# Batch 0 cut into query parts of 256 and 320 rows in place of 384 and 192, and its feed-forward rows divided at 255 in place of 256

## The chip, the cores and the metric

The kernel runs on 1 core of one Trainium2 chip. The metric is the device time of one execution in microseconds (us), lower is better. Engines are named as in the profile: PE is TensorE (PEld its weight loads), DVE is VectorE, ACT is ScalarE, POOL is GpSimd, SP is SyncE, which issues the DMAs.

## The reference, cut to what matters

Top-k attention, then a gated feed-forward block with a convolution of three taps along the sequence. There are 8 batches, 8 heads, 576 rows, 64 columns per head, 32 kept scores; the feed-forward block has 512 model columns and 1024 inner ones.

```python
scores = scale * np.matmul(q, k.transpose(0, 1, 3, 2))
kth = np.partition(scores, -top_k, axis=-1)[..., -top_k:-top_k + 1]
scores = np.where(scores >= kth, scores, -1000000000.0)
attn = np.exp(scores - np.max(scores, axis=-1, keepdims=True))
x = np.matmul(attn / (np.sum(attn, axis=-1, keepdims=True) + 1e-09), v)   # heads side by side: (B, S, 512)
h = np.maximum(x @ w_in, 0.0)
conv_out = sum(conv_w[k] * hp[:, k:k + S, :] for k in range(3))            # hp: h with a zero row at both ends
out = (h * (1.0 / (1.0 + np.exp(-conv_out)))) @ w_out
```

## The kernel before, in words

**Tiles.** Heads go in pairs. The 576 queries of a batch are four blocks of 128 and one of 64. A tile is 128 query rows against all 576 keys for one head (the 64-row blocks of two pairs share tiles), so a batch has 36 tiles and the program 288. `PARTS` (line 65) gives the order inside a batch: blocks 0, 1, 2 for all four pairs (24 tiles), then block 3 and the 64 for all four pairs (12 tiles).

**The order of the work.** A Python loop, `iteration(it)`, writes the instructions of PE, ACT, DVE and POOL in their final order; each call is one tile step, with many tiles in flight. A tile n passes: scores on PE, then `evacuate` (ACT, L252) two steps before `chunk_ops` reads it; `chunk_ops` and `cand_ops` (DVE, L268 to L290: the largest values of seven pieces of the row); `sides` (ACT, L302); `flip` (POOL, L307, writes the tile's z); one step later `expo` (ACT, L314, which takes its shift from z); and one more step later `below` (DVE, L317, which reads z), `select` (DVE, L321) and `weigh` (DVE, L335); then transposes and products with v on PE. SP's DMAs are ordered by the framework's own scheduler.

**Weights.** In the first 33 steps the 64-bit weights are fetched in 33 blocks (block 0 the taps, 1 to 16 of w_in, 17 to 32 of w_out) and converted, one block a step: DVE cuts them (L162, then one step later L171), ACT works on them between (L165, L167), POOL ends the conversion (L176, L178, L179).

**Shared buffers.** Two rings of six buffers each, tags `x_hi` and `x_lo` of the pool `xp`, hold both the raw weight blocks of `load` (line 143, ten blocks ahead of use) and later the attention outputs of `normalise` (line 420: L424, L425 `x_hi`, L426 `x_lo` on POOL). Whoever takes a buffer waits until its last reader is done.

**Feed-forward.** `ROWS` (line 89) divides a batch's 576 rows into a group of 256 and one of 320. When all four pairs of a part are normalised, `ffn` queues 8 expansions (`Expand`: 12 matmuls, L456; the convolution on POOL, L489 to L503; tanh on ACT, L517; the gate on DVE, L525) and the contractions (`Contract`: a split of 128 rows on POOL, L588 and L592; matmuls L613). The first group needs one row more than it holds, since the convolution reaches a row further: 257 rows (258 columns are computed), for which two blocks don't do. Credits (`FEED`, `LEAN`, `PACE`, `FIRST`) set how many of these units a step takes. The last units run after the last tile.

```python
PARTS = ((0, 1, 2), (3, None))
ROWS = [(0, NI * TAIL), (NI * TAIL, S)]
feed = EARLY if state.blocks < BLOCKS else FEED if work[min(max(it, 0), NT - 1)].pc.part == 0 else LEAN
```

## Time and profile before

| What | Value |
|---|---|
| median of 3 runs | 1099.97 us (1098.80 to 1101.86) |
| the profiled execution | 1099.58 us, of which the span of the program is 1097.8 us |
| busy: DVE, PE | 1031.1 us (94%), 1022.0 us (93%) |
| busy: ACT, POOL | 956.1 us (87%), 934.0 us (85%) |
| DVE busy from 50 to 200 us | 149.65 of 150 us |
| mean granted TensorE clock of the span | 0.983 of full speed |

The profiled execution's own time is 1.8 us over its span, which leaves out what lies around the program. Sums further down are made against 1099.58 us. Shares of busy time are means over stages with different limits: a part with weight conversion, a long even part, and a tail without tiles, so a stretch is to be read by itself.

### The profile page before, as it was taken

To read this page: it belongs to the slowest core of one execution; us is meant where nothing else is said; L and a number is where in the kernel's file an instruction comes from. 1 tells how busy PE (TensorE), PEld (TensorE's weight loads), DVE (VectorE), ACT (ScalarE), POOL (GpSimd) and SP (SyncE) were. 2 spreads that over 40 slices of the span, in tenths; PEclk is the share of its full clock that TensorE was granted. 3 is DMA by queue.
4 is the path that set the end of the run, shared out by engine and by line. 5 is a ranking of instruction groups with operands and counts; after the bars stand their busy time and mean duration, and the time that the engine had idled before them with its cause. 6 is when DMAs were issued, how large, how long until landed. Compare 5 with 4: busy or idle time off the path is not lost.

```text
span 1097.8 us, 27626 instructions
## 1 busy us (share of the span) xinstructions
PE 1022.0 (93%) x7890; PEld 761.9 (69%) x7890; DVE 1031.1 (94%) x5792; ACT 956.1 (87%) x2417; POOL 934.0 (85%) x1224
## 2 busy tenths in 40 slices
PE   6777798999989999999999999999999999999997
PEld 3444476766767777776777777776777767776895
DVE  7999999999999999999999999999999999999670
ACT  6888899989999998989999998989999999899551
POOL 6879779988889989899989989899988989899610
PEclk9988899999999999999999999999999999999999
DMA  9241222123212222222311322312311332221101
GB/s 298 90 127 65 69 60 79 48 78 116 72 48 79 85 70 79 77 74 86 96 44 60 119 64 65 94 57 93 93 59 49 98 95 63 65 69 45 40 19 43
DMA packets 71154, 85.96 MB, mean 78 GB/s; under 512 B 12848, under 2 KB 45904, under 8 KB 70992
## 3 DMA queue, kind: packets, MB, share of 16 engines
q1 hardware_dynamic: 70992, 84.10, 24.4%
q8 instruction: 65, 1.06, 0.4%
q14 instruction: 97, 0.79, 0.2%
HBM read 74.48 MB, written 9.58 MB: 77 GB/s over the span
## 4 chain that ended last, share of the span: by engine, by line
PE 57%; DVE 29%; ACT 10%; issue 1%; POOL 1%; DMA 0%; SPq 0%; ACTq 0%; POOLq 0%; DVEq 0%
PE mc L613 13%; PE me L456 12%; PE pt L347 9%; PE mixed L379 8%; DVE cand L268 8%; PE s L246 7%; DVE e L335 7%; DVE z L317 5%; DVE cand L290 2%; ACT weights_ps L314 2%; ACT side L302 2%; PE mixed L382 2%; DVE g L525 2%; PE mixed L230 2%; DVE rows L288 2%; PE weights_ps L613 2%
## 5 line engine op out<-in xcount | busy, mean ns | idle before, releaser
L268 DVE MAX8 cand<-rows 128x8 f32<-128x82 f32 (+1 forms) x2016 | 481.7, 241 | 0.0
L307 POOL TENSOR_TENSOR z<-rows,side 128x579 f32<-128x579 f32 x288 | 347.5, 1207 | 63.2 <-ACT side L302 55.6
L314 ACT ACTIVATE weights_ps<-rows,z 128x576 f32<-128x576 f32 x288 | 220.1, 764 | 22.2 <-DVE e L335 11.8
L335 DVE SCALAR_TENSOR_TENSOR e<-rows,kth,weights_ps 128x576 f32<-128x576 f32 x288 | 231.6, 804 | 0.3
L456 PE MATMUL me<-x_hi,wi 128*128 128x258 f32 (+1 forms) x952 | 227.4, 310 | 2.9 <-ACT g L470 2.8
L302 ACT ACTIVATE side<-rows 128x576 bf16<-128x576 f32 x288 | 223.5, 776 | 0.0
L347 PEld LDWEIGHTS pt<-ident,e 128*128 128x128 f32 x1152 | 123.7, 143 | 139.8 <-issue 21.1
L317 DVE MAX8 z<-z 128x8 f32<-128x576 f32 x288 | 213.9, 743 | 0.0
L613 PE MATMUL mc<-wo,split 128*128 128x512 f32 x732 | 199.2, 404 | 0.5 <-ACT o L629 0.5
L347 PE MATMUL pt<-ident,e 128*128 128x128 f32 x1152 | 193.0, 291 | 5.4 <-DVE e L335 5.0
L355 ACT COPY pT<-pt 128x512 f32<-128x512 f32 x256 | 153.1, 598 | 45.4 <-PE pt L347 44.9
L246 PE MATMUL s<-k,q 64*128 64x512 f32 x512 | 169.9, 671 | 3.1 <-ACT rows L252 3.0
L252 ACT COPY rows<-s 128x512 f32<-128x512 f32 x288 | 166.7, 579 | 5.7 <-PE s L246 4.2
L379 PE MATMUL mixed<-pT,vn 128*64 128x128 f32 (+1 forms) x2560 | 167.1, 275 | 0.0
L456 PEld LDWEIGHTS me<-x_hi,wi 128*128 128x128 f32 x952 | 161.8, 189 | 4.3 <-ACT g L470 4.3
L379 PEld LDWEIGHTS mixed<-pT,vn 128*64 128x64 f32 x2560 | 132.3, 141 | 17.4 <-issue 1.4
L613 PEld LDWEIGHTS mc<-wo,split 128*128 128x128 f32 x732 | 128.6, 189 | 21.6 <-POOL t L503 0.7
L456 PE MATMUL me<-x_lo,wi 128*128 128x258 f32 (+1 forms) x476 | 142.0, 298 | 0.0
L489 POOL TENSOR_SCALAR t<-g,cr 128x256 f32<-128x256 f32 (+1 forms) x228 | 116.5, 511 | 0.0
L288 DVE MAX8 rows<-cand 128x8 f32<-128x21 f32 x576 | 106.3, 185 | 0.0
L503 POOL TENSOR_TENSOR t<-t,t 128x256 f32<-128x256 f32 (+1 forms) x114 | 91.4, 802 | 9.5
L456 PEld LDWEIGHTS me<-x_lo,wi 128*128 128x128 f32 x476 | 90.9, 191 | 0.0
(126 smaller groups left out, 1695.7 us busy)
## 6 DMA issues: line engine op xcount, KB each, us to landing
vn<-in_v_main_dram SPq DMA_DIRECT2D x64, 256.0 KB
k<-in_k_dram SPq DMA_DIRECT2D x32, 384.0 KB
k<-in_k_dram SPq DMA_DIRECT2D x32, 352.0 KB
out_dram<-o SPq DMA_DIRECT2D x26, 256.0 KB
q<-in_q_dram SPq DMA_DIRECT2D x32, 192.0 KB
rb<-row SPq DMA_DIRECT2D x64, 96.0 KB
q<-in_q_dram SPq DMA_DIRECT2D x32, 160.0 KB
raw<-in_w_in_dram SPq DMA_DIRECT2D x16, 256.2 KB
```

The source lines that it names most:

```text
L246: nc.tensor.matmul(s_ps[h], lhsT=qx[d, at:at + P], rhs=kx[d, keys], start=True, stop=True)
L252: nc.scalar.copy(out=x[:, at:at + MAIN], in_=s_ps[t.h])
L268: yield lambda c=c, at=at, n=n: nc.vector.max(out=t.cand[:, c:8 * CHUNKS:CHUNKS], in_=t.x[:, at:at + n])
L302: nc.scalar.activation(out=t.side[:, 2:S + 2], in_=t.x, func=AF.Sign, scale=-OVER, bias=t.row[:, 7:8], accum_out=t.cnt)
L307: nc.gpsimd.tensor_tensor(t.z[:, 8:S + 11], t.row[:, 6:S + 9], t.side, ALU.mult)
L314: nc.scalar.activation(out=e_ps, in_=t.x, func=AF.Exp, scale=scale, bias=t.shift)
L317: nc.vector.max(out=t.z[:, 0:8], in_=t.z[:, 10:S + 10])
L335: nc.vector.scalar_tensor_tensor(out=t.e, in0=t.x, scalar=kth[:, t.n:t.n + 1], in1=e_ps, op0=ALU.is_ge, op1=ALU.mult, accum_out=t.pc.sums[ ...
L347: nc.tensor.transpose(tp[:, i * P:(i + 1) * P], t.e[:, o + i * P:o + (i + 1) * P], ident)
L379: nc.tensor.matmul(a[r, 0:st.w], lhsT=st.pc.vn[:, h, i], rhs=st.unit.pT[:, st.half[h], i, c], start=(i == 0), stop=False)
L456: nc.tensor.matmul(mm[:, 0:w], lhsT=wt, rhs=xx, start=(n == 0), stop=(n == len(ops) - 1))
L613: nc.tensor.matmul(mm[0:m], lhsT=x[:, i], rhs=wo[:, e, f], start=start, stop=stop)
```

## The change

Batch 0 alone gets another plan, `OPENING`: blocks 0 and 1 for all four pairs first (16 tiles), then blocks 2, 3 and the 64 (20 tiles). Its feed-forward rows are divided at 255: a group of 255 rows, which with one row more needs exactly the 256 of the two blocks, and one of 321. A contraction of 128 rows may now take its rows from two groups (127 of the first and 1 of the second for rows 128 to 255 of batch 0), and the next batch's first group waits for that contraction's split as well. Other batches stay as they were. Lines of the changed kernel are 15 to 20 higher: L186 is the L171 of before, L193 and L194 are L178 and L179, L323 is L307, L333 is L317, L337 is L321, L351 is L335, L440 to L442 are L424 to L426, L472 is L456.

```diff
 PARTS = ((0, 1, 2), (3, None))
+OPENING = ((0, 1), (2, 3, None))
...
-    ROWS = [(0, NI * TAIL), (NI * TAIL, S)]
+    CUT = {PARTS: NI * TAIL, OPENING: 2 * P - 1}
+    def parts_of(b):
+        return OPENING if b == 0 else PARTS
+    def rows_of(b, part):
+        return [(0, CUT[parts_of(b)]), (CUT[parts_of(b)], S)][part]
...
     def fetch(pc):
-        last = None in PARTS[pc.part]
+        last = pc.part == 1
         for nm, src, a, z, w in (("k", k, 0, S + 3 * TAIL if last else S + 2 * TAIL, S + 3 * TAIL),
-                                 ("q", q, pc.c0, S + P if last else pc.c1, WIDE)):
+                                 ("q", q, pc.c0, MAIN + P if last else pc.c1, max(WIDE, QW))):
...
-            s_lo, s_hi = ROWS[part]
+            s_lo, s_hi = rows_of(b, part)
...
-            if self.two:
-                srcs = [(0, TAIL, ends[self.b][:, fs]), (TAIL, P, self.gs["g"][:, fs, c0:c0 + TAIL])]
-            else:
-                srcs = [(0, P, self.gs["g"][:, fs, c0:c0 + P])]
+            srcs = [(0, TAIL, ends[self.b][:, fs])] if self.two else []
+            a, r = TAIL if self.two else 0, self.r
+            for gs, part, n in self.of:
+                c0 = gs["at"] + r - rows_of(self.b, part)[0]
+                srcs.append((a, a + n, gs["g"][:, fs, c0:c0 + n]))
+                a, r = a + n, r + n
...
-        if any(o.part == e.part and o.b < e.b for o in unready) or (state.it < state.due and not tail):
+        if any(e.part in o.parts and o.b < e.b for o in unready) or (state.it < state.due and not tail):
...
-        for part, blocks in enumerate(PARTS):
+        for part, blocks in enumerate(parts_of(b)):
```

**POOL, while weights are converted.** Here z is a tile's flipped row, xt a pair's attention output, x_hi and x_lo its two halves in the shared rings, scratch and wo belong to a weight block, and a name's number is its buffer or tile. Before, from the conversion of block 22 on:

```order
L176 TENSOR_TENSOR scratch_130<-scratch_130 128x256 [waits DVE_49]
L178 TENSOR_SCALAR wo_64<-scratch_130 128x256 [waits Pool_49]
L179 TENSOR_TENSOR wo_64<-scratch_130,wo_64 128x256 [waits Pool_49]
L307 TENSOR_TENSOR z_1202<-rows_108,side1_113 128x579 [waits DVE_49,Activation_49]
L424 TENSOR_TENSOR xt0_542<-xt0_542,rb_929 128x384 [waits DMAHW5_49,DMAHW4_49]
L176 TENSOR_TENSOR scratch_130<-scratch_130 128x256 [waits DVE_49]
L178 TENSOR_SCALAR wo_64<-scratch_130 128x256 [waits Pool_49]
L179 TENSOR_TENSOR wo_64<-scratch_130,wo_64 128x256 [waits Pool_49]
L307 TENSOR_TENSOR z_1253<-rows_108,side0_109 128x579 [waits DVE_49,Activation_49]
L425 TENSOR_SCALAR x_hi_1196<-xt0_542 128x384 [waits DMAHW6_49]
```

And in the changed kernel, where the first batch's second pair is normalised, from the conversion of block 21 on:

```order
L191 TENSOR_TENSOR scratch_130<-scratch_130 128x256
L193 TENSOR_SCALAR wo_64<-scratch_130 128x256 [waits Pool_49]
L194 TENSOR_TENSOR wo_64<-scratch_130,wo_64 128x256 [waits Pool_49]
L323 TENSOR_TENSOR z_1181<-rows_108,side0_109 128x579 [waits DVE_49,Activation_49]
L441 TENSOR_SCALAR x_hi_1005<-xt0_766 128x256 [waits DVE_49,Activation_49]
L442 TENSOR_TENSOR x_lo_1006<-xt0_766,x_hi_1005 128x256 [waits DMAHW7_49,DMAHW1_49,Pool_49]
L191 TENSOR_TENSOR scratch_130<-scratch_130 128x256
L193 TENSOR_SCALAR wo_64<-scratch_130 128x256 [waits Pool_49]
L194 TENSOR_TENSOR wo_64<-scratch_130,wo_64 128x256 [waits Pool_49]
L323 TENSOR_TENSOR z_1234<-rows_108,side1_113 128x579
```

The normalisation of the first pairs moved forward by some six conversions, and its x_hi now waits for DVE and ACT. Which instruction it waits for is told by the count in the built program: x_hi_1003 and x_lo_1004, of the first pair, lie where raw blocks 20 and 21 lay, and x_hi_1005 lies where raw64_682 lay, block 24, three blocks ahead of the block 21 that POOL has just converted; it waits for L186 of block 24 on DVE. Before, x_hi_1196 took the place of block 22, which POOL had converted ahead of it.

**DVE, at that L186.** The rows of the changed kernel from L186 of block 24 (raw64_682) to the reading of z_1234, the z that stands behind the waiting x_hi on POOL; cand, second and hot are a tile's largest values, mc and e2 go with a weight block and a tile's exponentials:

```order
L186 SCALAR_TENSOR_TENSOR scratch_130<-raw64_682,mc_131 128x256 [waits Activation_49]
L304 MAX rows_108<-cand_1199 128x8 [waits DVE_49]
L284 MAX cand_1250<-rows_108 128x8
L177 TENSOR_SCALAR mc_131<-raw64_727 128x256 [waits DMAHW5_49,DVE_49]
L337 SCALAR_TENSOR_TENSOR hot_1269,kth_67<-weights_ps_97,cnt_1126,z_1181 128x10 [waits Activation_49]
L351 SCALAR_TENSOR_TENSOR e2_1224,sums_1153<-rows_108,kth_67,weights_ps_97 128x576 [waits DVE_49,PE_49]
L304 MAX rows_108<-cand_1250 128x8 [waits DVE_49]
L306 MATCH_REPLACE cand_1250<-rows_108,cand_1250 128x21 [waits DVE_49]
L333 MAX z_1234<-z_1234 128x8 [waits Pool_49]
```

(Repeated L284 rows between them are left out.) The order of these rows is that of before; what moved is the POOL row that L333 waits for, which now stands behind a wait for L186.

**What does not move.** On each of the four engines the first pass of the two programs is the same list of instructions from one place on: on DVE from its 1413th row in both, after the same 84 tiles; the rows ahead of that place are the same kinds and counts in both but for widths. On DVE 12 gates of 256 columns and 7 of 320 become 7 of 255, 5 of 256 and 7 of 321, which are 5312 columns in both. POOL has four small operations more (2 casts and 2 differences of 128 by 4). On PE the first expansion stands after 26 groups of tile transposes in place of 32.

## Rows read from the trace of the kernel before

**Rows 1.** The page: the span, and the busy time of the engines.

```profile
span 1097.8 us, 27626 instructions
PE 1022.0 (93%) x7890; PEld 761.9 (69%) x7890; DVE 1031.1 (94%) x5792; ACT 956.1 (87%) x2417; POOL 934.0 (85%) x1224
```

**Rows 2.** Busy time by stretch: the stretch in us, its length, busy us (and instructions) of PE, PEld, DVE, ACT, POOL, the mean granted TensorE clock (1.00 is 2.4 GHz), the DMA engines' busy share and GB/s.

```profile
50.00:100.00 50.00, 36.16 (x224) 22.46 (x224) 49.93 (x271) 44.55 (x115) 41.01 (x54) 0.82 0.27 82
100.00:150.00 50.00, 39.62 (x317) 27.36 (x315) 49.86 (x290) 43.91 (x113) 37.97 (x49) 0.87 0.29 91
150.00:200.00 50.00, 46.45 (x408) 36.16 (x405) 49.86 (x290) 47.83 (x124) 47.71 (x70) 1.00 0.17 52
200.00:250.00 50.00, 47.41 (x352) 33.49 (x352) 49.23 (x284) 45.54 (x112) 45.17 (x53) 1.00 0.25 77
250.00:300.00 50.00, 48.38 (x411) 36.33 (x409) 49.25 (x290) 46.27 (x123) 44.05 (x60) 1.00 0.30 95
1050.00:1100.00 50.00, 40.33 (x197) 33.94 (x195) 16.95 (x35) 15.10 (x32) 0.00 (x0) 0.96 0.10 34
```

**Rows 3.** The waits of DVE (who waited, for whom, us in total, times, the longest): one row from 7.5 to 200 us, then two from 200 to 330 us.

```profile
DVE mc L162 <- DMA raw<-in_w_in_dram: 1.7, 1, 1.7
DVE hot L321 <- ACT weights_ps L314: 0.6, 1, 0.6
DVE hot L321 <- ACT weights_ps L517: 0.5, 1, 0.5
```

**Rows 4.** The timeline at the start (start us, duration us, engine, line, operation, and in brackets the idle time before and what ended it), and the page's slices with what the DMAs moved, 27.4 us each.

```profile
1.19 0.42 SPq L211 DMA_DIRECT2D q<-in_q_dram  x1
7.36 0.43 DVE L162 TENSOR_SCALAR mc<-raw 128x256 uint32<-128x256 uint32 x1 [1.66 <-DMA raw<-in_w_in_dram]
9.47 0.43 DVE L171 SCALAR_TENSOR_TENSOR scratch<-raw,mc 128x256 uint16<-128x256 uint16 x1
10.05 0.73 POOL L176 TENSOR_TENSOR scratch<-scratch 128x256 uint32<-128x256 uint32 x1 [3.95 <-DVE scratch L171]
...
GB/s 298 90 127 65 69 60 79 48 78 116 72 48 79 85 70 79 77 74 86 96 44 60 119 64 65 94 57 93 93 59 49 98 95 63 65 69 45 40 19 43
```

**Rows 5.** The timeline of POOL around a conversion and a normalisation.

```profile
91.77 0.51 POOL L425 TENSOR_SCALAR x_hi<-xt 128x384 fp32r<-128x384 f32 x1
92.24 0.73 POOL L176 TENSOR_TENSOR scratch<-scratch 128x256 uint32<-128x256 uint32 x1
...
94.24 1.20 POOL L307 TENSOR_TENSOR z<-rows,side 128x579 f32<-128x579 f32 x1
95.40 1.00 POOL L426 TENSOR_TENSOR x_lo<-xt,x_hi 128x384 fp32r<-128x384 f32 x1
```

**Rows 6.** The timeline of DVE: L171 of block 24, then a later tile step (that of rows 5) and the next.

```profile
82.63 0.42 DVE L171 SCALAR_TENSOR_TENSOR scratch<-raw,mc 128x256 uint16<-128x256 uint16 x1
...
94.21 0.43 DVE L171 SCALAR_TENSOR_TENSOR scratch<-raw,mc 128x256 uint16<-128x256 uint16 x1
96.83 0.74 DVE L317 MAX8 z<-z 128x8 f32<-128x576 f32 x1
98.04 0.43 DVE L171 SCALAR_TENSOR_TENSOR scratch<-raw,mc 128x256 uint16<-128x256 uint16 x1
98.96 0.22 DVE L321 SCALAR_TENSOR_TENSOR hot<-weights_ps,cnt,z 128x10 f32<-128x10 f32 x1
100.71 0.74 DVE L317 MAX8 z<-z 128x8 f32<-128x576 f32 x1
```

**Rows 7.** The timeline of ACT in that tile step.

```profile
95.59 0.43 ACT L167 ACTIVATE scratch<-raw 128x256 uint32<-128x256 uint32 x1
96.33 0.75 ACT L314 ACTIVATE weights_ps<-rows,z 128x576 f32<-128x576 f32 x1 [0.30 <-DVE e L335]
```

**Rows 8.** Groups of POOL with shapes kept apart (busy us, mean ns of one | idle us before).

```profile
L426 POOL TENSOR_TENSOR x_lo<-xt,x_hi 128x384 fp32r<-128x384 f32 x32 | 32.2, 1005 | 2.5
L426 POOL TENSOR_TENSOR x_lo<-xt,x_hi 128x192 fp32r<-128x192 f32 x32 | 19.5, 610 | 1.8
L425 POOL TENSOR_SCALAR x_hi<-xt 128x384 fp32r<-128x384 f32 x32 | 16.5, 516 | 0.0
L425 POOL TENSOR_SCALAR x_hi<-xt 128x192 fp32r<-128x192 f32 x32 | 11.6, 364 | 2.2
L588 POOL TENSOR_SCALAR split<-ends 128x256 fp32r<-128x256 f32 x6 | 2.4, 404 | 0.0
L465 POOL MEMSET g<- 128x8 f32 x8 | 0.9, 114 | 0.0
```

**Rows 9.** Short stretches with the granted TensorE clock, columns as in rows 2.

```profile
115.00:120.00 5.00, 5.00 (x32) 3.57 (x30) 5.00 (x28) 3.90 (x12) 4.34 (x7) 0.57 0.02 5
120.00:125.00 5.00, 3.10 (x21) 2.53 (x21) 5.00 (x30) 4.82 (x13) 3.57 (x6) 0.78 0.27 77
125.00:130.00 5.00, 3.51 (x30) 1.98 (x26) 5.00 (x31) 3.46 (x11) 2.06 (x3) 0.88 0.46 136
130.00:135.00 5.00, 4.10 (x35) 2.65 (x35) 4.93 (x31) 4.89 (x13) 4.52 (x6) 1.00 0.49 158
```

**Rows 10.** Expansions on PE: the first matmul of the first one in the timeline, and 12 matmuls of one unit in the chain that ended last (start us, us).

```profile
140.32 0.36 PE L456 MATMUL me<-x_hi,wi 128*128 128x258 f32 x1
1036.11 1.44 PE s L456 x12
```

More of the change, by code (lines that the diff above doesn't have):

```diff
@@ L75, in attend_and_feed @@
     exact = finish is None
+    pt_bufs = PTB - 1 if exact else PTB
     v_main, v_tail = v
@@ L88, in attend_and_feed, with width @@
     scale = 1.0 / float(D) ** 0.5
-    ROWS = [(0, NI * TAIL), (NI * TAIL, S)]
-    SMAX = max(e - a for a, e in ROWS)
-    WIDE = max(sum(TAIL if i is None else P for i in blocks) for blocks in PARTS)
-    SUMS = 2 * max(sum(1 if i is None else 2 for i in blocks) for blocks in PARTS)
+    CUT = {PARTS: NI * TAIL, OPENING: 2 * P - 1}
[3 more added lines that the diff above has]
+        return [(0, CUT[parts_of(b)]), (CUT[parts_of(b)], S)][part]
+    def width(blocks):
+        return sum(TAIL if i is None else P for i in blocks)
+    PLANS = (PARTS, OPENING)
+    WIDTHS = [max(width(plan[part]) for plan in PLANS) for part in range(2)]
+    WIDE = max(WIDTHS)
+    QW = max(MAIN + P - width(plan[0]) for plan in PLANS)
+    GROUPS = [max(CUT.values()), S - min(CUT.values())]
+    SMAX = max(GROUPS)
+    SUMS = 2 * max(sum(1 if i is None else 2 for i in blocks) for plan in PLANS for blocks in plan)
     const = ctx.enter_context(tc.tile_pool(name="const", bufs=1))
@@ L243, in scores @@
                     r = slice(half_of(one, h) * D, (half_of(one, h) + 1) * D)
-                    nc.tensor.matmul(s_ps[one.h][r], lhsT=qx[d, at:at + TAIL], rhs=kx[d, keys], start=True, stop=True)
+                    c = at + half_of(one, h) * TAIL
+                    nc.tensor.matmul(s_ps[one.h][r], lhsT=qx[d, c:c + TAIL], rhs=kx[d, keys], start=True, stop=True)
                 else:
@@ L461, in emit @@
             if self.f == 0:
-                g = self.gs["g"] = moe.tile([P, NFT, n + 4], F32, name=f"g{self.part}")
+                g = self.gs["g"] = moe.tile([P, NFT, GROUPS[self.part] + 4], F32, name=f"g{self.part}")
                 self.gs["at"] = at
@@ L549, in attend_and_feed, with __init__ @@
         m = P
-        def __init__(self, b, part, s0, half, gs, box):
-            self.b, self.part, self.s0, self.gs, self.box = b, part, s0, gs, box
-            self.two = ROWS[part][1] - ROWS[part][0] - s0 == TAIL
+        def __init__(self, b, r, half, pieces, box):
+            self.b, self.r, self.of, self.box = b, r, pieces, box
+            self.all = [gs for gs, _, _ in pieces]
+            self.parts = [part for _, part, _ in pieces]
+            self.two = r + TAIL == S
             nf = NFT * TAIL // self.m
@@ L619, in emit @@
             m, mm = self.m, self.box.mm
-            r = ROWS[self.part][0] + self.s0
+            r = self.r
             if state.it > NT + 4:
@@ L641, in split_next @@
         c = next((c for c in unready if not hasattr(c, "hi")), None)
-        if c is None or c.gs.get("done", 0) < NFT or (state.late_splits >= 4 if state.it > NT + 4 else state.splits >= SPB):
+        if c is None or any(gs.get("done", 0) < NFT for gs in c.all) or (state.late_splits >= 4 if state.it > NT + 4 else state.splits >= SPB):
             return False
@@ L645, in split_next @@
         return True
+    groups = {}
     def ffn(b, part):
-        gs = {}
+        gs = groups[b, part] = {}
         expands.extend(Expand(b, part, f, gs) for f in range(NFT))
-        n = ROWS[part][1] - ROWS[part][0]
-        for s0 in range(0, n, P):
+        lo, hi = rows_of(b, part)
+        for r in range(lo // P * P, S if part else hi // P * P, P):
+            if S - r == TAIL and b % 2 == 0:
+                unready.append(Keep(b, r, gs))
+                continue
+            pieces = [(gs, part, min(r + P, S) - max(r, lo))]
+            if r < lo:
+                pieces.insert(0, (groups[b, 0], 0, lo - r))
             box = Box()
-            if n - s0 == TAIL and b % 2 == 0:
-                unready.append(Keep(b, part, s0, gs))
-                continue
-            units = [Contract(b, part, s0, half, gs, box) for half in range(2)]
+            units = [Contract(b, r, half, pieces, box) for half in range(2)]
             contracts.extend(units)
```

18 lines of the change are left out of this document (9 added, 9 removed).

## The prediction

> **What bounds the kernel now.** I read the page's busy times first, then the busy time by stretch, then the waits of DVE, and last the order of the two programs. The page has DVE and PE close together, 94% and 93% of a span of 1097.8 us [rows 1], which names neither. The stretches do: from 50 to 200 us DVE is busy for all but 0.35 of 150 us while PE has 3.5 to 14 us free in each 50, and from 200 to 300 us DVE is still at 49.2 of 50 [rows 2]. The waits say the same: after the first weight block has landed, DVE waits for nothing worth a row until 200 us, and from there to 330 us for ACT alone, 0.6 and 0.5 us [rows 3]. Only in the last 50 us does PE carry the end alone [rows 2]. So ahead of 330 us a change is worth what it does to DVE's list of work and to DVE's waits, and nothing else.
>
> The change touches only that part. From the place after 84 tiles the four engines hold the same instructions in the same order in both programs, and ahead of it DVE has the same kinds and counts, its gates the same 5312 columns. The earlier start of batch 0's feed-forward work is thus given back: the next batch's work must wait for it, and by tile 84 both programs have done the same. The tail at the end is the same list, so an early gain on PE buys nothing there. What is left is one new wait, a smaller first transfer, and the clock of PE.
>
> **The change part by part.**
>
> *DVE's work: 0.* Same columns, same counts. DVE was never idle there, so the work can't be packed tighter either: what it could win back is the 1.1 us that it waits for ACT between 200 and 330 us [rows 3]. I take 0, because those waits follow how ACT's tanh and exponentials fall, which the change shifts without thinning; the bound is a gain of 1.1.
>
> *The moved normalisation: about +2.2 us.* The moved x_hi of the second pair lies where raw weight block 24 lay, and so waits for L186 of that block, three conversions ahead of where POOL is. Behind it on POOL, which works in order, stand x_lo, the conversion of block 22 and the next tile's z. Let time 0 be the end of that L186. I price what POOL then still has to do before that z, from rows of before:
> - waking POOL after DVE's L171: 9.47 + 0.43 = 9.90 to 10.05, 0.15 [rows 4];
> - x_hi and x_lo, 256 wide: between 364 and 516 ns, and between 610 and 1005 ns, for 192 and 384 [rows 8]; a third of the way up is 0.41 and 0.74, less some 0.04 that neighbours overlap (x_hi took 0.51, the next began after 0.47 [rows 5]): 0.37 and 0.70;
> - the conversion: 92.24 to 94.24, 2.00 [rows 5];
> - z: 1.20 [rows 5].
>
> The sum is 4.42. DVE reads a z 2.19 after L171's end (94.64 to 96.83 [rows 6]). So L333 comes 2.2 us late, and since DVE has no idle time to take that out of before 200 us, the end is 2.2 us later.
>
> Does it stop there? The next z is due one tile step on, 3.88 later (96.83 to 100.71 [rows 6]), and POOL needs 2.00 + 1.16 for it, so POOL is 0.7 ahead again. ACT's exponential, which takes its shift from the same z, waits as well: it would start 1.69 after time 0 (96.33 [rows 7]) and starts at 4.4, but its reader, L321, follows L317 by 2.13 [rows 6], thus at 6.5, and the exponential of 0.75 has ended at 5.2. ACT's last conversion operation of a block (L167) needs the scratch buffer that POOL frees at 3.2, ahead of the exponential. So one late z, once. The first pair's x_hi and x_lo wait also (for blocks 20 and 21), but POOL has z's in hand then: z follows at 0.15 + 0.70 + 2.00 + 1.20 = 4.05 after block 21's L186, and DVE wants it one whole step and 2.19 later, at 6.0. Nothing.
>
> The bounds: 0, if the buffer were free when POOL comes (nearest rows: x_hi of before follows its z without idle time [rows 5]); 4.4, if DVE had no step in hand and lost all that POOL does after the wait. I take 2.2, from rows of the very step.
>
> *The first transfer: -0.2.* Queries of the first pair shrink from 384 to 256 columns, 66 KB, and the weight block that ends DVE's last early wait lands behind them [rows 4]. At 298 GB/s of the first slice [rows 4] that is 0.2 us; bounds 0 and 0.35, the wait being partly latency.
>
> *Four small POOL operations: 0.* Each lies between the 114 ns of a small memset and the 404 ns of a cast of 256 [rows 8], 0.5 to 1.6 us in all; they fall past 250 us, where POOL has 5.9 of 50 us free [rows 2], with z's due a step later. With that cover gone they would cost up to 1.6.
>
> *SP: 0.* The DMA of the last weight block now waits for block 22's L186, and behind it on SP stand the second pair group's row sums and the keys of the fourth pair of the second part. Those keys are wanted some five tile steps of 3.83 us later (94.21 to 98.04 [rows 6]), far beyond the one step of waiting. The norms' rows are needed on POOL steps later, too.
>
> *Expansions six tiles earlier: 0 on DVE.* Their first matmul moves from 140.3 us [rows 10] to about 140.3 - 6 x 3.83 = 117 us. PE has room in 100 to 150 us [rows 2]; what is uncertain is its clock, below.
>
> Sum: 1099.58 + 2.2 - 0.2 = **1101.6 us** against the profiled execution, which lies 0.4 under the median of the runs (1099.97). That is 0.2% slower; a measurement of this kernel tells about 0.3%, 3.3 us, from no change, so I forecast no difference that can be told.
>
> **The rivals.**
> 1. *Slower: PE falls behind at 1.2 GHz.* The expansions now begin where the granted clock is 0.57 with PE busy 5.00 of 5.00 us [rows 9]. A unit of 1.44 us at full clock [rows 10] is 2.9 at half. Units come every 1.4 tile steps (`FIRST`), 5.4 us, so three begin before the clock is 1.00 at 130 us [rows 9]: 8.6 us against the two tile steps, 7.7 us, by which scores are evacuated ahead of DVE. It decides from the fourth unit at half clock; with five, 14.4 - 7.7 = 6.7 us are lost and the time is 1108.3. For it: 0.57. Against: the rows behind, 0.78, 0.88, 1.00, with less work than there will be. Chance 0.08.
> 2. *Slower: the late z is not made good.* ACT, held 2.7 us, makes the following tiles' rows late as well, and DVE loses twice: 4.4, 1103.8 and a little over. Against: ACT's 5 to 6 us free in 50 [rows 2]. Chance 0.08.
> 3. *No effect at all:* the wait ends in time, or what it costs is won back from the two waits for ACT: 1099.4. For: in 200 us no row shows DVE waiting for POOL. Chance 0.20.
> 4. *Faster: PE's clock.* The mean granted clock is 0.57, 0.78, 0.88 in 115 to 130 us [rows 9], which is 3.9 us of full clock not granted; were PE what limits these steps, expansions that raise it would give that back: 1099.6 - 3.9 = 1095.7. Against: DVE busy 5.00 of 5.00 in each of these rows. Chance 0.04. The Trainium skill ("TensorE: Matmul & The Clock Gate", section Terms) counts the penalty as throttled time by the share of pulses withheld. By that rule the stretch would be worth these 3.9 us; the trace here disagrees, since the engine that had no gap was DVE.
>
> **How the numbers follow.** Forecast 0.60; rivals 0.08, 0.08, 0.20, 0.04. The low end takes both gains, 0.35 and 1.1, without the stop: 1098.2; the high end the stop at its bound of 4.4: 1104.0. Outside lie rivals 1 and 4 and half of rival 2, 0.16. Faster by over 0.3% (under 1096.7) is rival 4 and a rest: 0.05. Slower by over 0.3% (over 1103.3) is rivals 1 and 2: 0.16. Within: 0.79.
>
> **What would show it.** In the profile after: x_hi's idle time on POOL (L441) before block 24's L186, near 83 us [rows 6], some 4 us, and behind it a DVE wait on L333 for POOL of about 2.2 us, once; no other new wait of DVE up to 330 us; its busy time unchanged within 1 us; the first expansion near 117 us; the gates and tiles after 330 us as before, 2 us later. Wrong would make it: no wait on L333; several of them; or DVE waiting for rows or for PE's results between 115 and 140 us at a low clock.

## Result: 0.55% slower, 1106.6 us against a forecast of 1101.6

The median of six runs of the changed kernel is 1106.58 us (1104.86 to 1107.11), beside 1100.37 us for the kernel before on the same chip (six runs, 1098.80 to 1101.86): a ratio of 1.0055 with a 95% interval of 1.0042 to 1.0068. That is slower by more than the measurement's 0.3%, and above the whole range that was forecast. The profiled execution took 1106.71 us, with a span of 1104.5 us against 1097.8. What lies outside the span grew too: 2.1 to 2.2 us in the six runs of the change, 1.8 in the profiled execution of before.

### The profile after

The page's first lines answer to [rows 1]. DVE does what it did (1031.9 us beside 1031.1), in a longer span.

```profile
span 1104.5 us, 27627 instructions
PE 1024.4 (93%) x7890; PEld 763.4 (69%) x7890; DVE 1031.9 (93%) x5792; ACT 955.0 (86%) x2417; POOL 938.6 (85%) x1228
```

The 50-us stretches, columns as in [rows 2]: PE, PEld, DVE, ACT, POOL busy, the granted clock, DMA.

```profile
50.00:100.00 50.00, 34.65 (x221) 21.74 (x222) 47.64 (x263) 42.02 (x108) 36.58 (x51) 0.82 0.34 106
100.00:150.00 50.00, 42.71 (x343) 30.59 (x341) 49.93 (x285) 45.89 (x121) 47.62 (x67) 0.88 0.14 44
150.00:200.00 50.00, 42.94 (x345) 31.02 (x344) 49.52 (x288) 44.54 (x114) 43.27 (x57) 0.97 0.21 60
200.00:250.00 50.00, 43.62 (x329) 32.15 (x328) 48.73 (x280) 45.60 (x114) 39.16 (x46) 0.93 0.22 68
250.00:300.00 50.00, 48.43 (x427) 36.33 (x427) 49.28 (x290) 45.63 (x119) 45.69 (x62) 1.00 0.30 92
300.00:350.00 50.00, 47.73 (x374) 36.34 (x373) 48.47 (x283) 46.28 (x117) 43.02 (x56) 1.00 0.16 54
```

DVE loses 2.3 us in one stretch (50 to 100 us), and smaller amounts from 150 to 250 us and from 300 to 350 (48.47 us busy, 49.93 before). Its waits from 10 to 380 us (us in all, times, longest), of the change and then of the kernel before:

```profile
DVE hot L337 <- ACT weights_ps L533: 2.8, 5, 1.1
DVE z L333 <- POOL z L323: 2.3, 1, 2.3
DVE hot L337 <- ACT weights_ps L330: 1.2, 3, 0.6
```

```profile
DVE hot L321 <- ACT weights_ps L517: 1.0, 2, 0.6
DVE hot L321 <- ACT weights_ps L314: 0.6, 1, 0.6
```

The middle row of the change is the wait that was forecast, once and of the forecast size. The two rows around it are not: DVE waits 4.0 us for ACT's tanh (L533) and exponential (L330) where it waited 1.6.

**Where the time went.** Both programs weigh the same 288 tiles in the same order of steps, so the end of the n-th weighing on DVE (L351, before L335) is a mark that can be laid beside the other's. The table gives by how much each stretch is longer than in the first profile of before, whose marks lie at 49.60 us (8th tile), 139.71 (32nd), 330.32 (88th), 1001.18 (280th) and 1097.75 (the end). The kernels under the first three rows are those of the experiments below. What the timed runs say stands in the last columns.

| Kernel | to 8th tile | 8th to 32nd | 32nd to 88th | 88th to 280th | behind | median us, runs | ratio to before, 95% |
|---|---|---|---|---|---|---|---|
| before, second profile | -0.18 | -0.03 | -0.07 | 0.00 | +0.59 | | |
| **change** | +0.36 | +2.31 | +2.90 | -0.78 | +1.94 | 1106.58, 6 | 1.0055 [1.0042, 1.0068] |
| change, second profile | +0.52 | +2.29 | +3.02 | -0.66 | +1.77 | | |
| normalisation later | +0.46 | -0.05 | +3.42 | -0.50 | +1.26 | 1104.87, 8 | 1.0038 [1.0027, 1.0048] |
| own rows | +0.31 | +2.30 | +2.51 | -0.72 | +0.75 | 1106.48, 5 | 1.0053 [1.0039, 1.0067] |
| both of these | +0.81 | -0.05 | +3.32 | -0.54 | +1.08 | 1104.23, 6 | 1.0032 [1.0020, 1.0044] |
| expansions held, two profiles | +0.35, +0.29 | +2.34, +2.28 | +1.05, +1.05 | -0.68, -0.75 | +0.42, +0.90 | 1105.80, 6 | 1.0055 [1.0043, 1.0067] |
| cut alone, four profiles | -0.59 to +0.44 | -0.04 to -0.01 | +1.38 to +1.81 | -0.75 to -0.50 | +0.19 to +2.60 | 1103.91, 11 | 1.0025 [1.0016, 1.0034] |
| cut alone, own rows | +0.26 | -0.01 | +0.65 | -0.61 | +2.70 | 1101.19, 11 | 1.0012 [1.0003, 1.0021] |
| order of blocks alone | -0.39 | -0.06 | -0.33 | -0.60 | +1.81 | 1099.95, 11 | 1.0000 [0.9991, 1.0009] |
| before, plain delay | +0.68 | +5.54 | +0.28 | -0.09 | +0.86 | 1105.80, 5 | 1.0049 [1.0036, 1.0062] |

The three stretches in the middle come again within 0.25 us when a kernel is profiled again, but for 0.43 in the cut alone; the first and the last do not. So the middle columns are the kernel's own, and a profile is read there rather than by its span.

**The late z.** POOL in the change, and DVE beside it:

```profile
91.67 0.41 POOL L441 TENSOR_SCALAR x_hi<-xt 128x256 fp32r<-128x256 f32 x1 [4.12 <-ACT side L318]
...
94.85 1.20 POOL L323 TENSOR_TENSOR z<-rows,side 128x579 f32<-128x579 f32 x1
```

```profile
91.08 0.42 DVE L186 SCALAR_TENSOR_TENSOR scratch<-raw,mc 128x256 uint16<-128x256 uint16 x1
...
96.08 0.76 DVE L333 MAX8 z<-z 128x8 f32<-128x576 f32 x1 [2.25 <-POOL z L323]
```

POOL stands idle 4.12 us ahead of x_hi. The row names ACT as the one that ended it, but x_hi starts 0.17 us after DVE's L186 has ended (91.50), which is the instruction that the built program makes it wait for; then follow x_lo, a conversion and the z, and DVE has waited 2.25 us. The next z is not late.

**The full PE.** Tiles 76 to 83 (the 77th to the 84th), first before, then in the change, columns as above. Then the matmuls of the expansions and of the contractions in that stretch of the change (PE, PEld, clock, DMA): 30 contraction matmuls, where before has 6 (1.55 us).

```profile
289.55:316.56 27.01, 24.65 (x208) 18.88 (x206) 27.01 (x158) 26.05 (x67) 23.69 (x34) 1.00 0.28 89
```

```profile
293.29:322.13 28.84, 28.84 (x227) 22.16 (x226) 27.38 (x158) 26.22 (x66) 24.34 (x35) 1.00 0.26 82
```

```profile
293.29:322.13 28.84, 7.65 (x53) 6.77 (x54) 1.00 0.26 82
293.29:322.13 28.84, 8.38 (x30) 5.14 (x30) 1.00 0.26 82
```

Before, DVE had no gap in 27.01 us. In the change PE has none in 28.84, and DVE has 1.46. The chain that ended last (start us, us) is PE alone here, for 14 us (me is written by expansions, mc by contractions):

```profile
295.98 0.59 PE pt L363 x4
...
296.81 1.40 PE mc L633 x6
...
300.37 1.44 PE me L472 x12
301.81 0.70 PE mc L633 x3
302.50 1.06 PE s L262 x4
...
304.15 1.40 PE mc L633 x6
...
307.71 1.43 PE me L472 x12
309.14 0.71 PE mc L633 x3
```

How it reaches DVE is to be seen a little later on ACT and then DVE: transposes behind the matmuls hold ACT 1.01 us, the exponential and the tanh behind it end late, and L337 waits 1.07 us.

```profile
315.08 0.59 ACT L371 COPY pT<-pt 128x512 f32<-128x512 f32 x1 [1.01 <-PE pt L363]
...
315.88 0.77 ACT L330 ACTIVATE weights_ps<-rows,z 128x576 f32<-128x576 f32 x1
316.68 0.48 ACT L533 ACTIVATE weights_ps<-t,cw 128x256 f32<-128x256 f32 x1
```

```profile
317.19 0.23 DVE L337 SCALAR_TENSOR_TENSOR hot<-weights_ps,cnt,z 128x10 f32<-128x10 f32 x1 [1.07 <-ACT weights_ps L533]
```

And where PE could have done it earlier, in the change, tiles 36 to 43 and tiles 52 to 63:

```profile
155.76:183.82 28.06, 21.00 (x173) 14.03 (x173) 27.65 (x162) 25.20 (x66) 23.27 (x31) 0.94 0.20 55
210.92:253.00 42.08, 35.70 (x273) 25.34 (x271) 41.13 (x238) 38.16 (x96) 32.34 (x38) 0.92 0.21 65
```

PE has 7.1 and 6.4 us free; before, in the same tiles, it was busy 24.57 of 27.24 and 39.80 of 41.46. The work that was put off comes right behind the first of these stretches. Tiles 44 to 51, before and in the change, and the wait of DVE that follows, after ACT has waited 0.61 us for transposes:

```profile
179.77:207.78 28.01, 26.20 (x211) 20.29 (x209) 27.79 (x161) 26.31 (x66) 26.84 (x38) 1.00 0.16 48
```

```profile
183.83:210.92 27.09, 27.09 (x208) 20.75 (x206) 26.70 (x157) 24.06 (x59) 22.96 (x29) 1.00 0.20 58
```

```profile
213.80 0.23 DVE L337 SCALAR_TENSOR_TENSOR hot<-weights_ps,cnt,z 128x10 f32<-128x10 f32 x1 [0.71 <-ACT weights_ps L533]
```

From the 32nd to the 88th tile DVE is idle for 3.9 us in the change and for 1.6 before. So 2.3 of the 2.9 us are waits; the other 0.6 are DVE's own operations, which take 189.6 us there in place of 189.0, and why was not separated.

The matmuls (expansion, contraction) counted in the built programs, each by the number of tiles whose transposes stand ahead of it on PE:

| Tiles | before | change | cut alone | own rows |
|---|---|---|---|---|
| 24 to 35 | 36, 0 | 96, 0 | 36, 0 | 96, 0 |
| 36 to 43 | 72, 0 | 12, 0 | 72, 0 | 12, 0 |
| 44 to 51 | 60, 0 | 48, 24 | 60, 0 | 48, 30 |
| 52 to 59 | 24, 36 | 36, 0 | 24, 24 | 36, 18 |
| 60 to 75 | 58, 54 | 58, 42 | 60, 51 | 58, 42 |
| 76 to 83 | 50, 6 | 50, 30 | 48, 21 | 50, 6 |

### The profile page after: what moved, and what is told of

It is laid out like the page before. It is cut to its first block, busy times and chain, and to the rows that moved or that the text cites. A ratio compares the mean times of both kernels' runs of the same rounds, so it can differ in the third digit from the quotient of the medians.

```text
span 1104.5 us, 27627 instructions
## 1 busy us (share of the span) xinstructions
PE 1024.4 (93%) x7890; PEld 763.4 (69%) x7890; DVE 1031.9 (93%) x5792; ACT 955.0 (86%) x2417; POOL 938.6 (85%) x1228
## 4 chain that ended last, share of the span: by engine, by line
PE 57%; DVE 30%; ACT 9%; POOL 2%; issue 1%; DMA 0%; SPq 0%; ACTq 0%; POOLq 0%; DVEq 0%
PE mc L633 13%; PE me L472 12%; PE pt L363 9%; PE mixed L395 8%; DVE cand L284 8%; PE s L262 7%; DVE e L351 7%; DVE z L333 5%; DVE cand L306 2%; ACT weights_ps L330 2%; PE mixed L398 2%; DVE g L541 2%; ACT side L318 2%; PE mixed L245 2%; DVE rows L304 2%; PE weights_ps L633 2%
## 5 line engine op out<-in xcount | busy, mean ns | idle before, releaser
L284 DVE MAX8 cand<-rows 128x8 f32<-128x82 f32 (+1 forms) x2016 | 482.9, 241 | 0.0
L323 POOL TENSOR_TENSOR z<-rows,side 128x579 f32<-128x579 f32 x288 | 346.9, 1205 | 56.4 <-ACT side L318 47.8
L330 ACT ACTIVATE weights_ps<-rows,z 128x576 f32<-128x576 f32 x288 | 220.3, 765 | 24.6 <-DVE e L351 12.1
L351 DVE SCALAR_TENSOR_TENSOR e<-rows,kth,weights_ps 128x576 f32<-128x576 f32 x288 | 231.7, 805 | 0.3
L472 PE MATMUL me<-x_hi,wi 128*128 128x322 f32 (+2 forms) x952 | 225.4, 309 | 0.8 <-ACT g L486 0.8
L333 DVE MAX8 z<-z 128x8 f32<-128x576 f32 x288 | 214.2, 744 | 2.7 <-POOL z L323 2.6
L472 PEld LDWEIGHTS me<-x_hi,wi 128*128 128x128 f32 x952 | 161.0, 190 | 1.9 <-ACT g L486 1.7
L472 PE MATMUL me<-x_lo,wi 128*128 128x322 f32 (+2 forms) x476 | 141.0, 296 | 0.0
L505 POOL TENSOR_SCALAR t<-g,cr 128x256 f32<-128x256 f32 (+3 forms) x228 | 116.0, 509 | 0.0
L519 POOL TENSOR_TENSOR t<-t,t 128x256 f32<-128x256 f32 (+3 forms) x114 | 91.2, 800 | 9.5
L472 PEld LDWEIGHTS me<-x_lo,wi 128*128 128x128 f32 x476 | 90.8, 191 | 0.0
```

What stands on the lines that cost most here:

```text
L284: yield lambda c=c, at=at, n=n: nc.vector.max(out=t.cand[:, c:8 * CHUNKS:CHUNKS], in_=t.x[:, at:at + n])
L323: nc.gpsimd.tensor_tensor(t.z[:, 8:S + 11], t.row[:, 6:S + 9], t.side, ALU.mult)
L330: nc.scalar.activation(out=e_ps, in_=t.x, func=AF.Exp, scale=scale, bias=t.shift)
L333: nc.vector.max(out=t.z[:, 0:8], in_=t.z[:, 10:S + 10])
L351: nc.vector.scalar_tensor_tensor(out=t.e, in0=t.x, scalar=kth[:, t.n:t.n + 1], in1=e_ps, op0=ALU.is_ge, op1=ALU.mult, accum_out=t.pc.sums[ ...
L472: nc.tensor.matmul(mm[:, 0:w], lhsT=wt, rhs=xx, start=(n == 0), stop=(n == len(ops) - 1))
```

## The experiments

Edits are against the changed kernel unless it is said otherwise.

**1. The normalisation later.**

```
-                norm_wait.append((it + NORM_LAG, st.pc))
+                norm_wait.append((it + NORM_LAG + (3 if st.pc is pcs[1] else 0), st.pc))
```

> The change, with the normalisation of the first two pairs of batch 0 held back by three tile steps, so that x_hi of the second pair reaches POOL after L186 of weight block 24 is done; nothing else is edited. Theory A (the loss is a sum of a start 0.35 us later, one late z of 2.25 us at 96 us, waits of DVE for ACT between 165 and 372 us that are 2.2 us more than before, and 1.2 us at the end): the wait of DVE on L333 for POOL is gone and nothing takes its place, 1106.6 - 2.2 = 1104.4 us. Rival (the late z is where a lack of POOL or ACT shows that would come out elsewhere without it): the wait moves to another line, 1106.6 us.

1104.87 us, 1.7 under the change. The wait is gone: on POOL the second pair's x_hi follows a z at once.

```profile
107.44 1.20 POOL L323 TENSOR_TENSOR z<-rows,side 128x579 f32<-128x579 f32 x1
108.61 0.40 POOL L441 TENSOR_SCALAR x_hi<-xt 128x256 fp32r<-128x256 f32 x1
```

The stretch from the 8th to the 32nd tile gives back 2.36 us, the next one loses 0.5 more. The term of the late z is shown; about a fifth of it was lost again behind it.

**2. Own rows.** The contraction of rows 128 to 255 no longer waits for the second group.

```
             if r < lo:
-                pieces.insert(0, (groups[b, 0], 0, lo - r))
+                pieces = [(groups[b, 0], 0, P)]
```

> The change, with one edit: the contraction of rows 128 to 255 of batch 0 takes all its 128 rows from the first group (its row 255 is there without its gate, so that one row of batch 0 leaves out the gate), and so waits for the first group alone. Its 24 matmuls then stand among tiles 48 to 59 on PE, as 24 of before stood among 52 to 63, in place of tiles 76 to 83. Theory A (in the change the contraction waits for the second group, and lands where the next batch's expansions fill PE, so that scores and transposes come late to ACT and the exponentials late to DVE): tiles 76 to 83 take 27.0 us as before, not 28.8, and the time is 1106.6 - 1.8 = 1104.8 us. Rival B (the waits for ACT come from the stretches at 1.2 GHz that the change has at 160 to 170 and 230 to 250 us): tiles 76 to 83 stay near 28.8 us, or the loss moves to tiles 48 to 59, and the time stays at 1106.6 us.

1106.48 us, as the rival said. Tiles 76 to 83 are back at 27.00 us with PE at 24.62, as theory A said, but the same matmuls, now in tiles 48 to 59, cost nearly as much there, as the rival's second branch said: tiles 52 to 63 took 43.52 us, 41.46 before and 42.08 in the change. The rival's cause, the stretches at 1.2 GHz, does not fit: five waits of DVE for ACT, 2.5 us in all, lie between 206 and 239 us, the clock is 1.00 up to 240 us, and PE has no gap from 200 to 235 us. The rows are tiles 52 to 63, the stretch without a gap, and tiles 76 to 83.

```profile
210.85:254.37 43.52, 38.40 (x295) 27.66 (x292) 41.41 (x238) 38.53 (x96) 33.54 (x39) 0.96 0.23 70
200.00:235.00 35.00, 35.00 (x272) 27.04 (x271) 32.76 (x190) 30.46 (x76) 31.34 (x37) 1.00 0.19 54
294.67:321.67 27.00, 24.62 (x208) 18.85 (x206) 27.00 (x158) 26.03 (x67) 23.61 (x34) 1.00 0.27 87
```

So the late contraction decides where 1.8 us are lost, but taking its wait away gives back only 0.4 of the 2.9 us from the 32nd to the 88th tile: with the expansions of the second group running beside it, an earlier place is hardly cheaper. The same holds for the change itself: each of its seven waits of more than 0.15 us for ACT between the 32nd and the 88th tile lies where the clock is 1.00. My theory was one cause short.

**3. Both.** 

> Both edits of the two runs ahead: the normalisation held back by three tile steps, and the contraction of rows 128 to 255 fed from the first group (one row without its gate). Theory A: the two terms add, 1106.6 - 2.2 - 1.8 = 1102.6 us, and what is left over 1100.4 is the start (0.35), some 0.6 of waits for ACT between 160 and 215 us and the end (1.2). Rival B: 1104.4 us, the wait for z alone gone.

1104.23 us: the z alone is gone, as rival B had it; 3.32 us stay between the 32nd and the 88th tile.

**4. The cut alone.** The order of blocks of before for all batches; `cut_of` is 255 for batch 0 and 256 for the others.

```
-        return OPENING if b == 0 else PARTS
+        return PARTS
...
-        return [(0, CUT[parts_of(b)]), (CUT[parts_of(b)], S)][part]
+        return [(0, cut_of(b)), (cut_of(b), S)][part]
```

> The block order of before for all batches (blocks 0, 1, 2 first), with the cut of batch 0 alone at 255 in place of 256. No earlier normalisation, no earlier expansion; the contraction of rows 128 to 255 waits for the second group, as in the change, and of the contraction matmuls 21 stand among tiles 76 to 83 where before has 6 and the change 30. Theory A: no wait on L333, the waits for ACT come among tiles 72 to 87 at somewhat more than half of the change's 1.8 us: 1100.4 + 1.1 = 1101.5 us. Rival B (clock and the earlier start): the cut by itself costs nothing, 1100.4 us. Rival C (odd widths of 255 and 321 make the operations on DVE, ACT or POOL longer): DVE's gates, ACT's tanh or POOL's taps of the first batch take longer per column than before, and the waits lie all over 140 to 250 us.

1103.91 us, more than theory A or rival B said, and in two groups of runs. Its own loss in the middle is 1.4 to 1.8 us, somewhat more than the 1.1 of theory A; the rest lies at the end (experiment 8) and, for 0.3 us, outside the span. Rival C fails on the rows of the change: gates of 321 and 255 columns take what 320 and 256 take. The kernel of experiment 6 has these widths too, at a ratio of 1.0000.

```profile
L541 DVE SCALAR_TENSOR_TENSOR g<-weights_ps,g 128x320 f32<-128x320 f32 x42 | 19.9, 474 | 0.0
L541 DVE SCALAR_TENSOR_TENSOR g<-weights_ps,g 128x256 f32<-128x256 f32 x39 | 15.9, 408 | 0.0
...
L541 DVE SCALAR_TENSOR_TENSOR g<-weights_ps,g 128x321 f32<-128x321 f32 x7 | 3.3, 475 | 0.0
...
L541 DVE SCALAR_TENSOR_TENSOR g<-weights_ps,g 128x255 f32<-128x255 f32 x7 | 2.8, 405 | 0.0
```

**5. The cut alone, own rows.** The edit of 2 on the kernel of 4. 

> The cut at 255 with the block order of before, and the contraction of rows 128 to 255 fed from the first group alone (row 255 of batch 0 without its gate). The widths are those of the change (255, 256, 321); the order of matmuls is that of before in every group of four tiles. Theory A (the 3.5 us of the cut alone come from the contraction that waits for the second group): 1100.4 us. Rival C (the odd widths): 1103.9 us as with the cut alone.

1101.19 us, nearer to theory A than to rival C, and tiles 76 to 83 lose nothing. The contraction's wait is worth about 0.9 of the cut's 1.55 us (mean of four). The 0.65 left are for the most part one wait of DVE for a z at 188 us (0.55 us); why POOL is late there was not separated, and the next kernel, with the same widths, does not have it.

**6. The order of blocks alone.** Edits 1 and 2 together, and two more:

```
-            state.due = max(state.due, state.it)
+            state.due = max(state.due, state.it, 35)
...
-  ("q", q, pc.c0, MAIN + P if last else pc.c1, max(WIDE, QW))
+  ("q", q, pc.c0, MAIN + P if last else max(pc.c1, WIDE), max(WIDE, QW))
```

> The change with its four suspected parts undone and only the order of the blocks left: normalisation of the first two pairs three steps later, expansions of the first group not before step 35 (as before), contraction of rows 128 to 255 from the first group alone (row 255 without its gate), and the first fetch of queries 384 columns wide as before. Theory A: nothing is left, 1100.4 us; first weight block after 7.4 us as before, no wait on L333, waits for ACT to 372 us within 0.6 us of before. Rival D (the block order itself costs, by its transfers, row sums or normalisations): up to the 1104.2 us of the run with two parts undone.

1099.95 us, a ratio of 1.0000: theory A holds as a whole. From 10 to 380 us DVE waits three times, 0.6 and 0.5 us for ACT and 0.2 for a z (L333, where theory A had none). Beside experiment 3, which differs by the held expansions (and by the first fetch, which acts at the start), the stretch from the 32nd to the 88th tile falls from +3.32 to -0.33 us.

**7. The expansions held.** The change with the `state.due` edit alone.

> The change with one edit: the expansions of the first group of batch 0 not before step 35, as before; the early normalisation with its late z, the cut and the contraction's wait stay. The matmuls then stand in every group of four tiles as in the cut alone, but for one unit one group earlier. Theory A (the earlier start leaves PE without feed-forward work in tiles 36 to 43, and the work that is then late is packed into fuller steps): tiles 32 to 87 cost 1.8 us over before, as with the cut alone, in place of 2.9, so the median is 1106.6 - 1.1 = 1105.5 us. Rival (the early start costs nothing, the cut and the clock all): 1106.6 us.

The median, 1105.80 us, is 0.8 under the change, the six runs spread from 1103.36 to 1109.17, and the interval of the ratio is that of the change: the time does not show the gain. The two profiles do: +1.05 us twice from the 32nd to the 88th tile, where the change has +2.90 and +3.02. So the early start costs 1.9 us there, more than the 1.1 of theory A, and the cut with its late contraction 1.05. Of the 1.9 us, 1.5 lie in tiles 32 to 63 and 0.35 behind them. Tiles 76 to 83 took 28.01 us, with PE busy for 26.64, so 1.0 of the 1.8 us that the change loses there comes without the early start. The two shares hold for this order of undoing them and do not add up in every other: with the contraction's wait undone first, 2.51 us (3.32 without the late z) stay, and the order of blocks alone has -0.33.

> The change with the expansions of the first group held to step 35, a second profile. The first was its fastest execution (1103.4 us; the others 1104.8 to 1106.7). Its matmul order in tiles 32 to 87 is that of the cut alone, so whatever separates the slower executions of the cut alone separates these too: theory F by tile 87 (3.7 us over before in the first profile, 5 to 6 then), rival G behind tile 279, rival H between.

1103.65 us: the middle is the same within 0.1 us, and this was again one of its faster executions, so it does not decide between the three.

**8. The end, and why runs of one kernel differ.** Two repetitions, then two more of the cut alone.

> The cut alone, once more, for a second profile: its eleven runs lie at 1101.4 to 1102.4 us (four) and at 1103.5 to 1104.4 us (seven), the former with a mean clock of 0.979 to 0.985, the latter with 0.976 to 0.980. If this execution is one of the slower ones, theory E (the stretches at 1.2 GHz fall at other places of the same program from execution to execution, and cost time only where PE is what DVE waits for) has it with more low stretches than the first profile, and with the lost time in tiles 72 to 87 or behind tile 279. Rival: the lost time lies elsewhere, for instance in the transfers at the start.

1100.92 us, faster than all before it.

> The change, once more, for a second profile: its profile loses 0.35 us at the start and 1.2 us between tile 279 and 287, where the low stretch of the clock lasts 7 us against 3.5 in the profile of before. Theory E: the waits up to tile 279 come again within 0.5 us (z at 2.3 us, tiles 76 to 83 at 28.8 us); the 1.2 us at the end come again only if the low stretch lasts 7 us again, otherwise the time is near 1105.3 us. Rival: the end is a fixed part of the change and comes again with a short stretch too.

1106.83 us: the waits come again within 0.5 us, z at 2.25 us, and the end is long again, with the clock low for as long again.

> The cut alone, a third profile. Its two profiles so far lie at 1101.9 and 1100.9 us and lose 0.8 to 1.1 us over before up to tile 279, yet seven of its eleven timed runs lie at 1103.5 to 1104.4 us with a lower mean clock (0.976 to 0.980). Theory F (PE has less free time in the stretch where the late contraction is missing, the granted clock falls there in some executions, and PE then enters tiles 68 to 87 late): an execution of the slower group shows low stretches between 220 and 260 us and two to three us lost by tile 87. Rival G: all of the difference lies behind tile 279. Rival H: the clock falls in the even part, behind tile 95.

> The cut alone, a fourth profile, as the third: theory F has the loss of the slower executions by tile 87 with low stretches between 220 and 260 us, rival G behind tile 279, rival H between tile 95 and 279. If both further profiles are of the faster group, the cause of the slower one stays open.

1102.74 and 1103.93 us. Rival G holds in the main: the ends are 99.0 and 99.2 us behind the 280th tile, 97.5 and 96.8 in the two faster ones; up to there the four differ by 1.05 us, nearly all of it at the start. Theory F and rival H fall. Where the end is longer, TensorE's granted clock is low for longer behind 1016 us, after a stretch in which PE waits for the last normalisations (once for 1.7 us for POOL's x_hi). The fastest of the four and then the slowest, columns as above:

```profile
1016.00:1018.00 2.00, 0.86 (x5) 0.52 (x5) 1.93 (x9) 1.94 (x8) 1.92 (x3) 1.00 0.40 144
1018.00:1020.00 2.00, 2.00 (x42) 1.88 (x41) 1.86 (x7) 1.23 (x4) 1.71 (x2) 0.60 0.14 36
1020.00:1022.00 2.00, 2.00 (x12) 2.00 (x11) 0.14 (x1) 0.89 (x4) 1.92 (x4) 0.54 0.16 42
1022.00:1024.00 2.00, 2.00 (x18) 1.83 (x17) 1.36 (x5) 1.64 (x5) 0.02 (x1) 1.00 0.70 179
```

```profile
1016.00:1018.00 2.00, 0.39 (x1) 0.19 (x1) 1.97 (x10) 1.97 (x8) 1.92 (x3) 0.89 0.36 133
1018.00:1020.00 2.00, 1.80 (x22) 1.57 (x24) 1.83 (x8) 1.87 (x5) 1.72 (x3) 0.50 0.14 39
1020.00:1022.00 2.00, 2.00 (x30) 1.88 (x27) 0.80 (x3) 0.00 (x0) 1.92 (x4) 0.50 0.14 36
1022.00:1024.00 2.00, 2.00 (x11) 2.00 (x10) 0.09 (x1) 1.46 (x4) 0.69 (x1) 0.50 0.53 119
1024.00:1026.00 2.00, 2.00 (x16) 1.84 (x16) 1.65 (x5) 1.20 (x4) 0.00 (x0) 0.90 0.24 77
```

Over the sixteen profiles with the same list of instructions behind the 280th tile, the mean clock from 1000 to 1040 us is 0.96 in eight and 0.91 in eight; the ends are 96.6 to 97.8 us in the former (mean 97.2) and 97.4 to 99.3 in the latter (mean 98.4). Up to the last tile the two groups lie apart: 26.9 to 27.5 us from the 280th to the 288th tile (mean 27.3) against 27.8 to 28.7 (mean 28.4). What follows takes 69.4 to 70.7 us in both, and what makes it differ stays open.

The Trainium skill ("TensorE: Matmul & The Clock Gate", section Terms) counts the penalty as the throttled time by the share of pulses withheld. Worked out by that rule for the two groups of rows above (2 us each by what is missing to 1.00) that is an estimated 1.7 and 3.4 us, a difference of 1.7; up to the last tile these two profiles took 27.4 and 28.7 us, a difference of 1.3, so the rule gives the direction and about the size here.

**9. A plain delay.** The kernel before with seven more MAX8 on DVE at tile 18.

```
-        nc.vector.max(out=t.z[:, 0:8], in_=t.z[:, 10:S + 10])
+        for _ in range(8 if t.n == 18 else 1):
+            nc.vector.max(out=t.z[:, 0:8], in_=t.z[:, 10:S + 10])
```

> The kernel before, with the MAX8 of L317 of tile 18 done eight times in place of once: seven more operations of some 0.75 us, 5.2 us of DVE, and the same results. Nothing else moves. Theory E (in the change the end is longer, 98.5 us behind tile 279 against 96.6 in the profile of before, because all that comes before is 5 us late and the low stretch of the clock behind 1017 us then falls on other matmuls): the delay and as much at the end, 1100.1 + 5.2 + 1.4 = 1106.7 us. Rival (the end is a matter of the execution, not of the delay): 1105.3 us, with ends of 96.6 to 99.3 us as the profiles so far have them.

1105.80 us, 5.1 over the before beside it, for a delay of 5.54: the rival. Being late does not by itself lengthen the end, by the medians; the one profile has an end of 97.5.

> The kernel before, once more, for a second profile. Its first profile has the shortest end of all so far: 96.6 us behind tile 279, with a granted clock of 0.96 from 1000 to 1040 us; six profiles with 0.96 there have 96.6 to 97.8 us, six with 0.91 have 97.4 to 99.3, whatever the kernel. Theory E, as it stands after the plain delay (the end is a matter of the execution): up to tile 279 the same times within 0.7 us, the start apart, and an end of 96.6 to 97.8 us with 0.96, or 97.4 to 99.3 with 0.91. Rival (the kernel before has the short end by its own, and the change lost 1.9 us there): 96.6 us again.

1099.89 us, 0.96 and an end of 97.2: theory E in the form it then had.

**10. The gate behind the weighing.** The waits for tanh suggested a version of the kernel before that might beat both: tanh always to its SBUF tile (`alone = False`), and the `gates` loop moved behind `weigh(tD)`.

> The kernel before with two edits that the waits point at: tanh writes its own SBUF tile in place of PSUM (so that L321, which waits for the last writer of the shared PSUM tile, waits for the exponential and not for the tanh behind it), and the gate stands behind the weighing in place of ahead of it. Theory A (DVE waits 14.7 us in 35 places for a tanh that follows the exponential it needs, and a tanh is 0.46 to 0.53 us): those waits lose that much each where they are longer, some 9 to 14 us less in all, about 1089 us. Rival (tanh only ends last; ACT is late for other reasons, and what is not waited there is waited at the next step): 1100 us, or above it for operands in SBUF on ACT and DVE (20 to 40 ns an operation, 2 x 95 of them: up to 6 us).

1108.96 us, a ratio of 1.0077 [1.0064, 1.0090]: slower. The waits did go, as theory A said (L321 waits 10.1 us in all in place of 21.5), but the gates got longer by more than the rival's price: 70.7 us in all, 50.0 before. Over the run, 320 and 256 columns; then from 1040 us on, where POOL is nearly done:

```profile
L525 DVE SCALAR_TENSOR_TENSOR g<-t,g 128x320 f32<-128x320 f32 x57 | 36.7, 645 | 0.9 <-ACT t L517 0.9
L525 DVE SCALAR_TENSOR_TENSOR g<-t,g 128x256 f32<-128x256 f32 x57 | 34.0, 606 | 1.6 <-ACT t L517 1.6
```

```profile
L525 DVE SCALAR_TENSOR_TENSOR g<-t,g 128x320 f32<-128x320 f32 x8 | 3.8, 491 | 0.9 <-ACT t L517 0.9
L525 DVE SCALAR_TENSOR_TENSOR g<-t,g 128x256 f32<-128x256 f32 x8 | 3.0, 417 | 1.6 <-ACT t L517 1.6
```

With one operand in PSUM they take 474 and 408 ns beside a busy POOL (experiment 4), so it is not the operation but the two SBUF operands beside POOL. Within this one run the gates of 256 columns say the same: 43 that an operation of POOL overlaps for more than half their time took 667 ns in the mean, the other 14 took 419. The Trainium skill ("SBUF — State Buffer", section Who interferes with whom) says that a DVE instruction with two SBUF inputs contends with a GpSimd instruction that reads SBUF; these rows agree. No version that was run beats the kernel before.

## Why the prediction was wrong

**The late z: right, +2.25 us for +2.2.** Its chain, its single occurrence and its size came out as worked out; with the normalisation held back it was gone. One detail was misread: the row of [rows 6] at 82.63 us is L171 of block 22, not 24, so the end of POOL's idle time was forecast near 83 us and came at 91.67, with DVE's wait ending at 96.08. The sum did not rest on it, since the price was worked out from the end of that instruction.

**The step that failed: "Expansions six tiles earlier: 0 on DVE", and behind it "what is left is one new wait".** I argued that an earlier start is given back by tile 84, where both programs hold the same rows, and took that for no cost. Equal at tile 84 means that the work in between was done, not that it was done as evenly. The first group's expansions now end at tile 35, and the second group's first one starts at 182.2 us, in tile 43, so PE has 7.1 us free in tiles 36 to 43. Then PE has no gap at all in tiles 44 to 51, and DVE waits for ACT, which waits for PE. The contraction of rows 128 to 255 waits for the second group and lands among the next batch's expansions, where the same happens again. The stretch from the 32nd to the 88th tile costs 2.9 us where I had 0: 1.9 by the early start, 1.05 by the cut with its late contraction (experiment 7); with these and the other suspected parts undone it costs nothing (experiment 6).

**"PE has room in 100 to 150 us" [rows 2]** was true and beside the point. The room has to be where the work arrives. [Rows 2] had the warning: PE busy for 48.4 of the 50 us from 250 to 300. I weighed the contraction's new wait nowhere.

**"DVE's work: 0": right.** 1031.9 us beside 1031.1. Its second half was wrong: I had the waits for ACT shifted and at best won back, and they grew from 1.6 to 4.0 us.

**The first transfer: -0.2 forecast, +0.4 measured.** In seven profiles with 256 columns the 8th tile ends 0.29 to 0.81 us late (mean 0.44), in ten with 384 from -0.78 to +0.68 (mean -0.03). Fewer bytes did not come sooner. Why is open.

**Rivals.** Rival 1 had the right chain (PE late, then ACT, then DVE) at the wrong place and for the wrong reason: from 115 to 140 us the clock was low as forecast and DVE had no wait; the loss came at 293 to 322 us with the clock at 1.00. Rivals 2, 3 and 4 did not happen. The first expansion came at 123.5 us, not near 117.

**What is accounted for.** Up to the 280th tile the two profiles of the change lose 4.8 and 5.2 us: 0.4 to 0.5 at the start, 2.3 by the z, 2.9 to 3.0 from the 32nd to the 88th tile, less 0.7. Those 0.7 are the 0.5 to 0.8 us that every kernel built on the changed file gains between the 88th and the 280th tile, and none built on the file before; the cause is open. The remaining 1.0 to 1.4 us of the 6.2 lie behind the 280th tile and outside the span. Outside it are 0.3: in every kernel whose contraction takes its rows from two groups an execution is in the mean 2.0 to 2.3 us longer than its span, in the others 1.8 to 1.9; why stays open. Behind the 280th tile the change was long in both profiles, before short in both, but the same list of instructions has run 96.6 to 99.3 us in kernels of every kind, and a plain delay did not bring it. Whether the change makes the long end more frequent stays open.

## What to carry to other kernels

Where an edit starts work earlier, do not stop at the step where the two programs meet again: count the work per step in between, on each engine, and look for the steps that got fuller, since room that an engine left unused earlier cannot be spent later. A unit that gets a second producer moves to wherever the later one ends, and its cost is set by what else runs there. Compare two profiles mark by mark along a common order of steps; spans alone hide a term of 2 us behind an end that differs as much from execution to execution.
